# Layer 1's low weight words: sixteen scalings that may run on GpSimd as well as on ScalarE

## The chip, the core and the metric

The kernel runs on one core of a Trainium2 chip. The time is device microseconds of one execution, as the median of several runs. The engines are named as the profile names them: PE is TensorE, PEld its weight loads, DVE is VectorE, ACT is ScalarE, POOL is GpSimd, and SP issues the transfers.

## What is computed

Windowed attention (4 sequences of 576 tokens, 8 heads of 64, window 64) is followed by two layers over all 2304 tokens with a model width of 512 and an inner width of 2048:

```
x = attention(q, k, v)                # 2304 x 512
h = maximum(x @ w1_in, 0); x = (h * h) @ w1_out
h = x @ w2_in; out = (h * cos(h)) @ w2_out
```

The weights reach the device as float64. The matmuls run in a split form: each operand is kept as a high part and a low part in a reduced float32 type, and three products (high·high, high·low, low·high) are added.

## The kernel before

**Weights.** Each layer's weights come in 16 blocks of 128 inner columns. A block is 1 MB of raw float64 in a tile `raw`, 128 partitions by 1024 numbers of two 32-bit words. `convert_w` (line 264) turns it into float32 and splits it. For layer 1 (`dst is None`) these are the steps of a block, all of 128x1024:

- load `raw` (L276, issued on SP);
- `o0`, the high words rescaled on ACT (L287);
- `o1`, the low words scaled by 2^-29 and rounded to integers, in place, on ACT (L245, with integer types in the trace);
- `o2`, the high words shifted left into `cw` on DVE (L299);
- `o4`, the two words added as integers on DVE (L303), which is the float32 weight;
- `hi`, the high part W rounded on ACT (L245, output fp32r);
- `lo`, the low part W by subtraction on DVE (L323).

Layer 2's blocks go through the same steps up to `o4` and are then stored to DRAM as float32 (`dst` is set); they come back later. Below, w0 to w15 are layer 1's raw blocks and W0 to W15 the finished ones.

**Items.** PE's work in layer 1 is a row of items. Item i multiplies one weight block with 256 or 512 tokens into `ph` (L877, 12 matmuls), ACT and DVE form the square `g` as two parts (L597, L601, L605 on ACT, L610 on DVE for the low part), and two items later PE multiplies `g_i` with the block's other half into `accA` (L624, L685). Items 0 to 11 are half units of 256 tokens over blocks 0 to 5, where tokens 0 to 255 start before tokens 256 to 511; from item 12 on, an item is 512 tokens with blocks 6 to 15. The attention of the first two token groups, n = 0 and 1, each in two head groups g, runs ahead of this. `mm` is its row minimum (L481 on DVE), `pb` the exponentials (L487 on ACT, L497 on DVE), T the transposes, O the result, and X the token matrix that `ph` reads.

**Order.** No engine chooses at run time. A planner (`Plan.run`) places every operation on one of the engines its table allows, by estimated costs in us, keys and free buffers, and the program is emitted in that order. `act_us`, `dve_us` and `pool_us` are its costs. Every engine works its instructions off in order. The planner puts an operation that two engines may take where it would be finished first. A different choice for one operation therefore changes the order of many others on all engines.

```
def pool_us(n, two=False):
    return 0.17 + n * (0.0021 if two else 0.00083)
...
        o0 = op({"ACT": act_us(2 * DM)}, key, c0, [o_ld], use=[rb])
        o1 = op({"ACT": act_us(2 * DM)}, key, c1, [o_ld], use=[rb])
```

`copy` (line 243) is the helper that carries out `o1` on whichever engine it is given: an activation on ACT, a `tensor_scalar` with two multiplications on POOL (line 247).

Of the kernel before, what the change touches and what calls it, by code (L numbers as in the profile page):

```python
# [28 lines left out]
def f32(ap):  # L29
    return ap.bitcast(F32)  # L30
# [55 lines left out]
class Plan:  # L86
# [6 lines left out]
    def op(self, engs, key, fn, deps=(), take=(), use=(), lat=None):  # L93
        if lat is None:
            lat = self.PE_LAT if "PE" in engs else self.LAT
        o = Op(engs, key, fn, [d for d in deps if d is not None], list(take), lat)
        o.seq = len(self.ops)
        self.ops.append(o)
        for b in (*take, *use):
            b.users.append(o)  # L100
        return o
# [61 lines left out]
def act_us(n, sbuf=True):  # L163
    return 0.05 + 0.093 * sbuf + n / 1200.0


def dve_us(n, fast=False):
    return 0.065 + n / (1920.0 if fast else 960.0)


def pool_us(n, two=False):
    return 0.17 + n * (0.0021 if two else 0.00083)
# [7 lines left out]
def kernel(  # L180
# [21 lines left out]
    DM = 512  # L202
# [22 lines left out]
    op = plan.op  # L225
# [11 lines left out]
    def dma(key, fn, nbytes, deps=(), take=(), use=(), n=1, order=()):  # L237
        return op({"SP": max(0.6 * n, nbytes / 360e3)}, key, fn, [*deps, *order], take, use, lat=2.2)
# [4 lines left out]
    def copy(e, o, i, scale=1.0):  # L243
        if e == "ACT":
            nc.scalar.activation(o, i, AF.Copy, scale=scale)  # L245
        elif e == "POOL":
            nc.gpsimd.tensor_scalar(o, i, scale, 1.0, ALU.mult, ALU.mult)
        elif scale == 1.0:
            nc.vector.tensor_copy(o, i)
        else:  # L250
            nc.vector.tensor_scalar(o, i, scale, None, ALU.mult)
# [9 lines left out]
    def new_w(wb, nm):  # L261
        wb.tile = wp.tile([P, 2, 2, DM], F32R, tag=f"W{wb.slot}", name=f"W_{nm}")

    def convert_w(src, j, key, after=None, dst=None, early=None):

        nm = f"{src.tensor.name}_{j}"  # L270
        raw, rb = {}, R["W"].buf()
        wb = R["W"].buf() if dst is None else None

        def ld(e):
            raw["t"] = wp.tile([P, 2, DM, 2], I32, tag=f"W{rb.slot}", name=f"raw_{nm}")
            nc.sync.dma_start(  # L276
                raw["t"].rearrange("p a n two -> p (a n two)"), src[j].bitcast(I32))

        o_ld = dma(key - 3 if early is None else early, ld, P * 2 * DM * 8, [after], [rb])

        def words():
            t = raw["t"].rearrange("p a n two -> p (a n) two")
            return t[:, :, 0], t[:, :, 1]

        def c0(e):
            hw = words()[1].bitcast(F32)
            nc.scalar.activation(hw, hw, AF.Prelu, scale=2.0**-112, alpha=-(2.0**32))  # L287

        def c1(e):
            lw = words()[0]  # L290
            copy(e, lw, lw.bitcast(U32), 2.0**-29)

        o0 = op({"ACT": act_us(2 * DM)}, key, c0, [o_ld], use=[rb])
        o1 = op({"ACT": act_us(2 * DM)}, key, c1, [o_ld], use=[rb])
        s, tb = {}, R["w"].buf()

        def c2(e):
            s["w"] = cv.tile([P, 2 * DM], I32, tag="w", name=f"cw_{nm}")
            nc.vector.tensor_scalar(s["w"], words()[1], 3, None, ALU.logical_shift_left)  # L299

        def c4(e):
            w = words()[1] if dst is None else s["w"]
            nc.vector.tensor_tensor(w, s["w"], words()[0], ALU.add)  # L303

        def w32():
            if dst is None:
                return raw["t"].bitcast(F32)[:, :, :, 1]
            return s["w"].bitcast(F32).rearrange("p (a n) -> p a n", a=2)

        o2 = op({"DVE": dve_us(2 * DM, True)}, key, c2, [o0], [tb], use=[rb])  # L310
        o4 = op({"DVE": dve_us(2 * DM)}, key, c4, [o2, o1], use=[rb, tb])
        if dst is None:
            tb = rb
        if dst is not None:
            return [dma(key, lambda e: nc.sync.dma_start(dst[j], w32()), P * 2 * DM * 4, [o4],
                        use=[tb])]

        def c5(e):
            new_w(wb, nm)
            copy(e, wb.tile[:, :, 0], w32())  # L320

        def c6(e):
            nc.vector.tensor_tensor(  # L323
                wb.tile[:, :, 1], w32(), f32(wb.tile[:, :, 0]), ALU.subtract)

        hi = op({"ACT": act_us(2 * DM)}, key, c5, [o4], [wb], [tb])
        lo = op({"DVE": dve_us(2 * DM)}, key, c6, [hi], use=[tb, wb])
        w_hi[j] = [hi, hi]
        w_lo[j] = [lo, lo]
        w_buf[j] = wb  # L330
# [580 lines left out]
    for j in range(NJ):  # L911
        convert_w(w1, j, -6.0 + 2.0 * (j if j < SK else 2 * j - SK), w_lo[j - 4][1] if j >= 4 else None, early=-96.0 + 1.5 * j if j < 2 else None)
# [11 lines left out]
    for i in range(len(items) + LAG + 1):  # L924
# [12 lines left out]
        if i in w2_at:  # L937
            j = w2_at[i]
            w2_done[j] = convert_w(w2, j, pos + 5.0, line[0], w2d)
# [80 lines left out]
```

## Time and profile before

| | |
|---|---|
| median of 3 runs | 886.24 us (886.02 to 887.07) |
| the profiled execution | 886.27 us, span 884.5 us |
| PE busy | 862.2 us, 97% of the span |
| ACT busy | 471.1 us, 53% |
| DVE busy | 509.8 us, 58% |
| POOL busy | 5.0 us, 1%, 25 instructions |

The span is the time from the first to the last instruction on the engines; 1.77 us of the execution lie around it. Busy time of PE counts a matmul from its start to a modelled end, so that a busy PE can still be a slow one; its granted clock stands beside it in some rows, as a share of 2.4 GHz.

### The profile page before, as it was taken

The numbers are of one execution on the slowest core, as the hardware profiler recorded it, in microseconds if no ns is written. First come the engines' busy times: TensorE is split into PE (matmuls) and PEld (weight loads), VectorE is DVE, ScalarE is ACT, GpSimd is POOL, SyncE is SP. The second block draws the span as 40 slices with busy tenths as digits, with TensorE's granted clock in tenths as the row PEclk, the third lists the DMA queues.
The fourth block names the chain that finished last, engine by engine and source line by source line (L and its number), as shares of the span: only waits on it lengthen the run. The fifth ranks groups of instructions, "written<-read, shape, count | busy, mean of one in ns | idle before, by whom it ended". The sixth has DMA issues, their size and how long they took to land.

```text
span 884.5 us, 13320 instructions
## 1 busy us (share of the span) xinstructions
PE 862.2 (97%) x5184; PEld 724.9 (82%) x5184; DVE 509.8 (58%) x1137; ACT 471.1 (53%) x953; POOL 5.0 (1%) x25
## 2 busy tenths in 40 slices
PE   5799999999999999999999999999999999999998
PEld 4698778998788888888888888888888888888897
DVE  4887845424444344434544966676667666766675
ACT  6899966746656655654433533344334333433444
POOL 2000000000000000000000000000000000000000
PEclk8799999999999999999999999999999999999999
DMA  8862236243334343225522200020002000200000
GB/s 329 362 228 96 84 117 223 97 168 137 132 130 161 111 177 128 96 72 160 221 96 95 84 13 1 0 86 11 1 1 95 1 1 1 71 1 1 15 34 25
DMA packets 22655, 85.40 MB, mean 97 GB/s; under 512 B 2368, under 2 KB 3392, under 8 KB 18496
## 3 DMA queue, kind: packets, MB, share of 16 engines
q1 hardware_dynamic: 22592, 84.55, 27.0%
q8 instruction: 41, 0.67, 0.3%
q14 instruction: 22, 0.18, 0.1%
HBM read 66.72 MB, written 17.83 MB: 96 GB/s over the span
## 4 chain that ended last, share of the span: by engine, by line
PE 91%; ACT 6%; DVE 1%; issue 1%; DMA 0%; ACTq 0%
PE ph L877 42%; PE accB L803 22%; PE accA L624 20%; PE S L468 2%; PE O L519 2%; PE T L505 2%; ACT raw_in_w_dram L287 1%; ACT W_in_w_dram L245 1%; ACT raw_in_w_dram L245 1%; ACT g L601 1%; ACT pb L487 1%; ACT r L597 0%; ACT r L605 0%; DMA qk<-in_qk_dram 0%; DVE pb L497 0%
## 5 line engine op out<-in xcount | busy, mean ns | idle before, releaser
L877 PE MATMUL ph<-X,W_in_w_dram 128*128 128x512 f32 (+1 forms) x1032 | 220.6, 360 | 2.5 <-ACT X L554 0.8
L877 PE MATMUL ph<-X,W 128*128 128x512 f32 (+1 forms) x960 | 209.8, 368 | 0.0
L803 PE MATMUL accB<-W,gb 128*128 128x512 f32 x864 | 208.8, 390 | 0.0
L624 PE MATMUL accA<-g,W_in_w_dram 128*128 128x512 f32 (+1 forms) x888 | 200.5, 370 | 0.0
L877 PEld LDWEIGHTS ph<-X,W_in_w_dram 128*128 128x128 f32 x1032 | 172.6, 190 | 32.4 <-issue 1.4
L877 PEld LDWEIGHTS ph<-X,W 128*128 128x128 f32 x960 | 169.3, 188 | 31.2
L803 PEld LDWEIGHTS accB<-W,gb 128*128 128x128 f32 x864 | 161.1, 188 | 32.9 <-ACT gb L780 0.2
L624 PEld LDWEIGHTS accA<-g,W_in_w_dram 128*128 128x128 f32 x888 | 153.2, 189 | 27.3 <-issue 0.9
L753 ACT ACTIVATE u<-ph,quarter 128x512 f32<-128x512 f32 (+1 forms) x80 | 51.7, 646 | 149.0 <-PE ph L877 149.0
L610 DVE TENSOR_TENSOR g<-r,g 128x512 fp32r<-128x512 f32 (+1 forms) x86 | 51.9, 604 | 107.8 <-ACT r L605 107.0
L757 DVE TENSOR_SCALAR u<-u 128x512 f32<-128x512 f32 (+1 forms) x80 | 32.0, 400 | 121.2 <-ACT u L753 121.2
L780 ACT ACTIVATE gb<-rr 128x512 fp32r<-128x512 f32 (+1 forms) x80 | 47.2, 590 | 83.9 <-DVE rr L775 83.9
L601 ACT ACTIVATE g<-r 128x512 fp32r<-128x512 f32 (+1 forms) x86 | 48.3, 561 | 80.3 <-PE accA L624 78.9
L597 ACT ACTIVATE r<-ph 128x512 f32<-128x512 f32 (+1 forms) x86 | 44.9, 522 | 51.6 <-PE ph L877 51.4
L487 ACT ACTIVATE pb<-pb,mm 128x128 f32<-128x128 f32 x144 | 55.9, 390 | 12.7 <-DVE mm L481 12.7
L772 ACT ACTIVATE u<-rr,hpi 128x512 f32<-128x512 f32 (+1 forms) x80 | 53.7, 672 | 0.3 <-DVE rr L768 0.2
L761 DVE SCALAR_TENSOR_TENSOR rr<-u,ph 128x512 f32<-128x512 f32 (+1 forms) x80 | 50.8, 635 | 2.5
L775 DVE TENSOR_TENSOR rr<-ph,u 128x512 f32<-128x512 f32 (+1 forms) x80 | 50.5, 631 | 1.4 <-ACT u L772 1.2
L783 DVE TENSOR_TENSOR gb<-rr,gb 128x512 fp32r<-128x512 f32 (+1 forms) x80 | 50.5, 632 | 1.0 <-ACT gb L780 1.0
L765 DVE SCALAR_TENSOR_TENSOR rr<-u,rr 128x512 f32<-128x512 f32 (+1 forms) x80 | 50.4, 631 | 0.3
L605 ACT ACTIVATE r<-r 128x512 f32<-128x512 f32 (+1 forms) x84 | 47.1, 561 | 2.7
L287 ACT ACTIVATE raw_in_w_dram<-raw_in_w_dram 128x1024 f32<-128x1024 f32 x32 | 36.7, 1147 | 1.7 <-DMA raw_in_w_dram<-in_w_dram 1.7
(63 smaller groups left out, 575.7 us busy)
## 6 DMA issues: line engine op xcount, KB each, us to landing
raw_in_w_dram<-in_w_dram SPq DMA_DIRECT2D x32, 1024.0 KB, 6.7
qk<-in_qk_dram SPq DMA_DIRECT2D x18, 576.0 KB, 4.1
v<-in_v_dram SPq DMA_DIRECT2D x18, 512.0 KB, 3.6
w_dram<-cw_in_w_dram SPq DMA_DIRECT2D x16, 512.0 KB, 3.8
w<-w_dram SPq DMA_DIRECT2D x8, 1024.0 KB, 5.0
x_dram<-x SPq DMA_DIRECT2D x18, 256.0 KB, 2.2
out_dram<-o SPq DMA_DIRECT2D x18, 256.0 KB, 2.0
xr<-x_dram SPq DMA_DIRECT2D x16, 256.0 KB, 2.7
```

The costliest lines, as they stand in the source:

```text
L487: nc.scalar.activation(t["pb"][:, e, r, i], t["pb"][:, e, r, i], AF.Exp, bias=t["mm"][:, e, r, i:i + 1], scale=-1.0, accum_out=t["sm"][:, ...
L601: nc.scalar.activation(t["g"][:, 0], t["r"], AF.Square)
L610: nc.vector.tensor_tensor(t["g"][:, 1], t["r"], f32(t["g"][:, 0]), ALU.subtract)
L624: nc.tensor.matmul(self.acc[i][:, k, :], w[:, 1, wl, m * P:m * P + P], t["g"][:, gl, :], start=(j == 0 and p == 0 and k == 0 and self.n > ...
L753: nc.scalar.activation(t["u"], ph()[:, 0:w], AF.Identity, bias=quarter, scale=INV_2PI)
L761: nc.vector.scalar_tensor_tensor(t["r"], t["u"], -C1, ph()[:, 0:w], ALU.mult, ALU.add)
L765: nc.vector.scalar_tensor_tensor(t["r"], t["u"], -C2, t["r"], ALU.mult, ALU.add)
L772: nc.scalar.activation(t["u"], t["r"], AF.Sin, bias=hpi)
L775: nc.vector.tensor_tensor(t["r"], ph()[:, 0:w], t["u"], ALU.mult)
L783: nc.vector.tensor_tensor(t["g"][:, 1], t["r"], f32(t["g"][:, 0]), ALU.subtract)
L803: nc.tensor.matmul(self.acc[m], t["g"][:, gl, m * P:m * P + P], w[:, 1, wl], start=(j == 0 and k == 0), stop=(j == NJ - 1 and k == 2))
L877: nc.tensor.matmul(t["ph"][:, 0:u.w], wb.tile[:, 0, wl, c * P:c * P + P], u.x(xl, c), start=(c == 0 and k == 0), stop=(c == NCC - 1 and k ...
```

## The change

Operation `o1` of layer 1's blocks may now run on POOL too, at a planner's cost of 0.17 + 1024 x 0.00083 + 0.15 = 1.17 us. Layer 2's blocks keep ACT alone.

```diff
-        o1 = op({"ACT": act_us(2 * DM)}, key, c1, [o_ld], use=[rb])
+        low = {"ACT": act_us(2 * DM)}
+        if dst is None:
+            low["POOL"] = pool_us(2 * DM) + 0.15
+        o1 = op(low, key, c1, [o_ld], use=[rb])
```

In the order that results, all sixteen of these operations stand on POOL and none on ACT, and lines behind the change move down by 3 (L299 becomes L302, and so on). SP issues the load of w5 one place earlier, ahead of an attention load. PE's order is the same up to the first `ph` and close to it for the items after. Three places follow.

DVE, from the sum of w2 to that of w3, while the attention of n = 1, g = 1 begins. Before (the rows left out are the other seven row minima of the same kind):

```order
L303 ISA raw_in_w1_dram_2_255<-raw_in_w1_dram_2_255,cw_in_w1_dram_2_415 128x1024x2
L323 TENSOR_TENSOR W_in_w1_dram_1_420<-raw_in_w1_dram_1_209,W_in_w1_dram_1_420 128x2x512
L481 ISA pb_1_1_424,mm_1_1_454<-S_1_1_0_425,row_mask_n_106 128x128
...
L323 TENSOR_TENSOR W_in_w1_dram_2_452<-raw_in_w1_dram_2_255,W_in_w1_dram_2_452 128x2x512
L493 TENSOR_SCALAR sm_1_1_455<-sm_1_1_455 128x4
```

With the change:

```order
L306 ISA raw_in_w1_dram_2_257<-raw_in_w1_dram_2_257,cw_in_w1_dram_2_406 128x1024x2
L613 TENSOR_TENSOR g_0_452<-r_0_431,g_0_452 128x256
L302 TENSOR_SCALAR cw_in_w1_dram_3_463<-raw_in_w1_dram_3_347 128x1024
L484 ISA pb_1_1_433,mm_1_1_471<-S_1_1_0_434,row_mask_n_106 128x128
...
L326 TENSOR_TENSOR W_in_w1_dram_2_458<-raw_in_w1_dram_2_257,W_in_w1_dram_2_458 128x2x512
L496 TENSOR_SCALAR sm_1_1_472<-sm_1_1_472 128x4
L497 RECIPROCAL sm_1_1_472<-sm_1_1_472 128x4
L500 TENSOR_TENSOR pb_1_1_433<-pb_1_1_433,sm_1_1_472 128x512
L306 ISA raw_in_w1_dram_3_347<-raw_in_w1_dram_3_347,cw_in_w1_dram_3_463 128x1024x2
```

The low part of g_0 and the shift of w3 now stand ahead of the eight row minima, and the low part of W1 has moved ahead of the sum of w2.

ACT, from the square of item 2 on, up to X for the second half's last head group. Before:

```order
L245 ACTIVATE raw_in_w1_dram_3_344<-raw_in_w1_dram_3_344 128x1024
L601 ACTIVATE g_2_556<-r_2_535 128x256
L605 ACTIVATE r_2_535<-r_2_535 128x256
L287 ACTIVATE raw_in_w1_dram_4_401<-raw_in_w1_dram_4_401 128x1024
L554 ACTIVATE X_83<-O_1_1_559 128x2x256
```

With the change:

```order
L604 ACTIVATE g_2_551<-r_2_545 128x256
L608 ACTIVATE r_2_545<-r_2_545 128x256
L287 ACTIVATE raw_in_w1_dram_4_408<-raw_in_w1_dram_4_408 128x1024
L287 ACTIVATE raw_in_w1_dram_5_455<-raw_in_w1_dram_5_455 128x1024
L287 ACTIVATE raw_in_w1_dram_6_499<-raw_in_w1_dram_6_499 128x1024
L557 ACTIVATE X_83<-O_1_1_571 128x2x256
```

Three rescalings of high words stand in a row before X, where one stood before.

DVE, behind X of the second half, up to g_6. With the change:

```order
L560 TENSOR_TENSOR X_83<-O_1_1_571,X_83 128x2x256
L302 TENSOR_SCALAR cw_in_w1_dram_5_596<-raw_in_w1_dram_5_455 128x1024
L326 TENSOR_TENSOR W_in_w1_dram_4_594<-raw_in_w1_dram_4_408,W_in_w1_dram_4_594 128x2x512
L306 ISA raw_in_w1_dram_5_455<-raw_in_w1_dram_5_455,cw_in_w1_dram_5_596 128x1024x2
L302 TENSOR_SCALAR cw_in_w1_dram_6_633<-raw_in_w1_dram_6_499 128x1024
L306 ISA raw_in_w1_dram_6_499<-raw_in_w1_dram_6_499,cw_in_w1_dram_6_633 128x1024x2
L613 TENSOR_TENSOR g_3_631<-r_3_608,g_3_631 128x256
L326 TENSOR_TENSOR W_in_w1_dram_5_642<-raw_in_w1_dram_5_455,W_in_w1_dram_5_642 128x2x512
L326 TENSOR_TENSOR W_in_w1_dram_6_660<-raw_in_w1_dram_6_499,W_in_w1_dram_6_660 128x2x512
L613 TENSOR_TENSOR g_4_670<-r_4_654,g_4_670 128x256
```

Before, the same stretch held less weight work between two items:

```order
L610 TENSOR_TENSOR g_3_615<-r_3_596,g_3_615 128x256
L323 TENSOR_TENSOR W_in_w1_dram_4_626<-raw_in_w1_dram_4_401,W_in_w1_dram_4_626 128x2x512
L303 ISA raw_in_w1_dram_5_461<-raw_in_w1_dram_5_461,cw_in_w1_dram_5_620 128x1024x2
L610 TENSOR_TENSOR g_4_652<-r_4_635,g_4_652 128x256
L299 TENSOR_SCALAR cw_in_w1_dram_6_677<-raw_in_w1_dram_6_492 128x1024
L323 TENSOR_TENSOR W_in_w1_dram_5_679<-raw_in_w1_dram_5_461,W_in_w1_dram_5_679 128x2x512
L610 TENSOR_TENSOR g_5_691<-r_5_675,g_5_691 128x256
```

Weight work has moved forward on DVE: between g_3 and g_12 it now holds nine low parts (L323), eight shifts (L299) and eight sums (L303).

## Rows read from the trace of the kernel before

**Rows 1.** Busy time per stretch: start:end, length, engines, PEclk, DMA share, GB/s.

```profile
30.00:40.00 10.00, 8.33 (x84) 7.11 (x81) 9.32 (x28) 8.66 (x25) 0.00 (x0) 0.84 0.80 320
...
50.00:60.00 10.00, 10.00 (x85) 10.00 (x84) 8.00 (x10) 9.87 (x18) 0.00 (x0) 1.00 0.46 164
...
150.00:884.50 734.50, 730.62 (x4025) 611.88 (x4017) 405.45 (x870) 347.01 (x678) 0.00 (x0) 1.00 0.22 75
```

**Rows 2.** PE in order of time: start, us, engine, line, [idle before <-releaser].

```profile
36.74 0.50 PE L877 MATMUL ph<-X,W_in_w_dram 128*128 128x256 f32 x2 [0.41 <-ACT W_in_w_dram L245]
38.00 1.10 PE L877 MATMUL ph<-X,W_in_w_dram 128*128 128x256 f32 x7 [0.76 <-DVE W_in_w_dram L323]
39.52 1.09 PE L505 MATMUL T<-ident,pb 128*128 128x128 f32 x4 [0.42 <-ACT pb L487]
...
46.47 0.38 PE L877 MATMUL ph<-X,W_in_w_dram 128*128 128x256 f32 x1 [0.79 <-ACT X L554]
47.32 0.86 PE L877 MATMUL ph<-X,W_in_w_dram 128*128 128x256 f32 x5 [0.46 <-DVE X L557]
...
53.77 1.60 PE L685 MATMUL accA<-g,W_in_w_dram 128*128 128x256 f32 x12
55.20 1.60 PE L877 MATMUL ph<-X,W_in_w_dram 128*128 128x256 f32 x12
...
83.59 2.88 PE L624 MATMUL accA<-g,W_in_w_dram 128*128 128x512 f32 x12
```

**Rows 3.** The same view, at 151 us, behind layer 1's last weight block.

```profile
151.49 1.60 PE L877 MATMUL ph<-X,W_in_w_dram 128*128 128x256 f32 x12
152.93 1.60 PE L624 MATMUL accA<-g,W_in_w_dram 128*128 128x256 f32 x12
```

**Rows 4.** PE alone per microsecond: start:end, length, busy (instructions), granted clock, DMA.

```profile
41.00:42.00 1.00, 1.00 (x7) 0.50 0.99 418
...
49.00:50.00 1.00, 1.00 (x11) 1.00 0.89 344
```

**Rows 5.** ACT in order of time: r_0's last step, one o1, then w4's rescaling and X.

```profile
34.23 0.42 ACT L605 ACTIVATE r<-r 128x256 f32<-128x256 f32 x1
...
42.16 1.14 ACT L245 ACTIVATE raw_in_w_dram<-raw_in_w_dram 128x1024 int32<-128x1024 uint32 x1
...
43.99 0.42 ACT L601 ACTIVATE g<-r 128x256 fp32r<-128x256 f32 x1 [0.69 <-PE accA L685]
...
44.76 1.18 ACT L287 ACTIVATE raw_in_w_dram<-raw_in_w_dram 128x1024 f32<-128x1024 f32 x1
45.83 0.59 ACT L554 ACTIVATE X<-O 128x512 fp32r<-128x512 f32 x1
```

**Rows 6.** DVE in order of time: first row minimum, W2's low part, X, then one block's steps.

```profile
34.74 0.28 DVE L481 CUSTOM_DVE_ANT_0 pb<-S,row_mask_n 128x128 f32<-128x128 f32 x1
...
36.72 1.23 DVE L323 TENSOR_TENSOR W_in_w_dram<-raw_in_w_dram,W_in_w_dram 128x1024 fp32r<-128x1024 f32 x1 [0.21 <-ACT W_in_w_dram L245]
...
46.58 0.68 DVE L557 TENSOR_TENSOR X<-O,X 128x512 fp32r<-128x512 f32 x1
...
59.26 0.69 DVE L299 TENSOR_SCALAR cw_in_w_dram<-raw_in_w_dram 128x1024 int32<-128x1024 int32 x1
60.01 0.43 DVE L610 TENSOR_TENSOR g<-r,g 128x256 fp32r<-128x256 f32 x1
61.05 1.23 DVE L323 TENSOR_TENSOR W_in_w_dram<-raw_in_w_dram,W_in_w_dram 128x1024 fp32r<-128x1024 f32 x1 [0.62 <-ACT W_in_w_dram L245]
62.39 1.23 DVE L303 CUSTOM_DVE_ANT_0 raw_in_w_dram<-raw_in_w_dram,cw_in_w_dram 128x2048 uint16<-128x2048 uint16 x1
```

**Rows 7.** POOL in order of time: three of its 25 instructions, all before 6.6 us.

```profile
4.17 0.20 POOL masks.py:197 MEMSET ident<- 128x128 f32 x1
4.44 0.29 POOL masks.py:199 TENSOR_SCALAR_AFFINE_SELECT ident<-ident 128x128 f32<-128x128 f32 x1
4.68 0.10 POOL L391 MEMSET hpi<- 128x1 f32 x1
```

## The prediction

> **What bounds the kernel now.** I read the busy time per stretch first, then PE in order of time. From 150 us on PE idles 3.9 us in 734.5, all of it behind the last matmul; between 50 and 60 us it does not idle [rows 1]. Up to the first `ph` the attention of the first tokens and its loads set the pace; PE's order there is unchanged, and the change takes nothing from that chain. So nearly all of PE's idle time that a weight conversion could cause lies between the first `ph` and 48 us: waits of 0.41, 0.76, 0.42, 0.79 and 0.46 us, together 2.84 us [rows 2]. In part of that stretch PE is also slow: at a granted clock of 0.50 it does 7 matmuls in a microsecond, at 1.00 it does 11 [rows 4].
>
> ACT is the engine that looks full: 9.87 us of 10 from 50 to 60 us [rows 1]. But it does not hold PE there. Twelve matmuls of 256 columns take 1.43 us in that stretch (53.77 to 55.20) [rows 2], and 1.44 us at 151 us, where layer 1's weight work is long over [rows 3]. PE runs at its own pace in both places. From 48 us on the kernel's end is therefore the moment at which the second half's `ph` gets its X (47.32 us [rows 2]) plus a sum of matmuls that the change leaves alone, unless something new makes PE wait.
>
> **What the change removes.** Sixteen instructions of about 1.14 us on ACT [rows 5], some 18 us of its time. Behind 48 us this is worth nothing by itself, because PE is the bound there. Ahead of 48 us three or four of them stand among the work that PE waits for, so I replayed the new order with the old durations. Consecutive DVE instructions overlap a little: eight row minima of 0.28 us took 36.72 - 0.21 - 34.74 = 1.77 us, so I take 0.07 off each duration as its step [rows 6].
>
> - Low part of W2. In the new order g_0's low part and the shift of w3 come ahead of the eight row minima. g_0 needs r_0, done at 34.23 + 0.42 = 34.65 us [rows 5]; with 0.36 and 0.62 us behind it, the minima begin at about 35.6 instead of 34.74 us, and W2's low part at 35.6 + 1.8 = 37.4 instead of 36.72 us [rows 6]. `ph` of item 2, which resumed at 38.00 us, resumes at about 38.6. The transpose behind it started at 39.52 us, late because of exponentials on ACT [rows 2]; now it starts at about 39.7, behind the matmuls. The wait for W2's high part (0.41 us) goes, and this one takes its place.
> - X of the second half. Its O is needed first, and the T and O before it are on PE as late as before. On ACT, w4's, w5's and w6's rescaling now come in a row ahead of it. w4's began at 44.76 us; without the 1.07 us step of `o1` that stood ahead of it and without the 0.69 us wait behind that, it begins at 43.0, and three steps of about 1.03 us end at 46.1 us; X then ends at 46.8 instead of 45.83 + 0.59 = 46.42 us [rows 5]. DVE has w4's sum before X's low part, which ends at about 47.7 us instead of 46.58 + 0.68 = 47.26 [rows 6]. What was saved on ACT is spent by work drawn forward.
>
> Term one: PE's uninterrupted run begins about 0.4 us later.
>
> **What it adds.** Sixteen POOL instructions of 128x1024, two words apart, from unsigned to signed integers. The trace has no such row. From below: a MEMSET grows from 0.10 us for 1 column to 0.20 for 128, which gives 0.91 us for 1024 columns by a straight line. From above: AFFINE_SELECT, which reads and writes, takes 0.29 us for 128 columns; with the same 0.10 us of start this gives 1.63 us for 1024 [rows 7]. The new operation reads and writes like the second but tests no pattern per element; I take 1.2 us. The GPSIMD Engine Reference of the Trainium skill, section 7, states about 1.9 cycles an element for reads of at most 8 bytes a step, at 1.2 GHz; the estimate from that page is 1.6 us, and with it the sum below would be 894.7 us. No run here shows it yet.
>
> As a producer POOL hides at any of these prices: it has nothing else to do and starts when a load has landed, where `o1` stood in line on ACT. What is open is whether it holds DVE up. In every stretch of [rows 1] POOL has no instruction, so no row shows the two at work on SBUF together. Bounds: such a pair costs DVE nothing, or the whole POOL instruction, 1.2 us. It costs nothing if the two have separate ways to SBUF. One row speaks for a shared one: DVE's shift passes 1024 words in 0.69 us, its subtraction 1024 in 1.23 [rows 6], so what DVE gets out of SBUF depends on the form of the instruction, and it sometimes takes more than one way. I take the upper bound for instructions that stand among DVE's weight steps, and keep zero as the rival.
>
> The page "SBUF — State Buffer" of the Trainium skill, section "SBUF: two separate sides", says that the two engines share a pair of ports as an exclusive lock, held for a whole instruction, against DVE instructions in a two-port mode or with two SBUF inputs. By that rule the upper bound holds, and L299, L303, L323 and L610 all come under it; without it the sum would end at term one, 886.7 us. Before this change the trace neither agrees nor disagrees.
>
> Term two, 29 to 48 us. Six loads land here, so about six POOL instructions run (w4 to w9). DVE is busy 9.32 us of 10 from 30 to 40 [rows 1], but in the replay it also has waits that swallow some: w2's sum ends near 33.4 us, and g_0 cannot start before 34.65 [rows 5]. I choose to count one of the six as late on the path, on W2's low part or the normalisation behind it: 1.2 us.
>
> Term three, behind 48 us. DVE now has its weight work packed. From X's low part (47.7) five steps come before g_3: 0.62 + 1.16 + 1.16 + 0.62 + 1.16 = 4.7 us, so g_3's low part ends at 52.8. PE wants it 6.45 us after X, as before (53.77 - 47.32 [rows 2]), at 54.15: slack 1.35 us. From g_3 to g_12 DVE has nine L323 of 1.16, eight L299 of 0.62, eight L303 of 1.16 and nine L610 of 0.36: 10.4 + 5.0 + 9.3 + 3.2 = 27.9 us, while PE takes 83.59 - 53.77 = 29.8 us [rows 2]. Spare: 1.9 us. The six POOL instructions that are left (w10 to w15) run in this stretch, as buffers come free. If each takes its 1.2 us out of DVE, 7.2 us stand against 1.35 + 1.9 = 3.25, and g's low parts reach PE 3.95 us late. PE does not make this up. Without turn-taking, term three is zero: the cover is that spare.
>
> **Sum.** 0.4 + 1.2 + 3.95 = 5.5 us on the profiled execution's 886.27 us (0.03 above the median of the runs): **891.8 us**. At the upper bound of 1.63 us a POOL instruction, with two on the early path: 0.4 + 3.3 + 6.5 = 10.2, 896.5 us. At no cost at all: 886.7 us.
>
> **Rivals.** About 0.2%, 1.8 us, is what a measurement of this kernel tells from no change.
>
> - *The cover holds* (0.30). POOL and DVE do not disturb each other, or only at L299, with the subtractions and sums free: eight shifts between g_3 and g_12 lose half a microsecond each at most, 4 us against a spare of 3.25. Time 886.7 us, from 885.5 to 888. For it: POOL has 99% of the span free, DVE has slack. Against: DVE is packed, so even small losses add up.
> - *Faster* (0.13). ACT relieved lets the conversions arrive early enough that PE's waits of 2.84 us between 36 and 48 us go, and PE, without these gaps, does not fall to clock 0.50 [rows 4]. This would be worth up to 2.84 us and, for that slow microsecond and its neighbours, an estimated 1.6 more: 881.9 us, or 883.4 with the waits alone. For it: ACT is named in two of the five waits. Against: the replay, where other work moves into each gap. It decides if the minima on DVE do not wait for g_0.
> - *Worse* (0.07). The POOL instruction costs 2.3 us (AFFINE_SELECT's 0.29 times eight) and DVE takes turns with it: term three is 6 x 2.3 - 3.25 = 10.6, with 0.4 and two of 2.3, about 15.6: 901.9 us.
> - That the scheduler leaves them on ACT is ruled out by the order.
>
> **How the numbers follow.** The forecast, turn-taking at 0.9 to 1.63 us, has a chance of 0.50: it spans about 888.5 to 896.5 us. Slower is that and the worst case, 0.57; within 0.2% is the cover, 0.30; faster is 0.13. The range runs from 884.6 to 897.0 us: it takes in the cover case with an error of the replay of 2 us, and leaves out the worst case and nearly all of the faster one, 0.19.
>
> **What would show it.** Right: POOL rows of about 1.2 us or longer beside DVE rows; L299, L303 or L323 longer than 0.69 and 1.23 us, or DVE idle before L303 for POOL; PE waits for DVE's g (L613) between 55 and 85 us; DVE close to 10 of 10 there. X's low part near 47.7 us or later. Wrong: DVE's durations as before under POOL's rows, PE without a wait behind 48 us (then 886.7), or PE's waits between 36 and 48 us gone (then less). A clock that falls at another place than around 41 us would move the start by up to 1.6 us either way.

## The result: 894.27 us, 0.9% slower, and the profile after

The changed kernel takes 894.27 us (median of 4 runs, 893.88 to 894.59) against 886.13 us for the kernel before on the same chip (4 runs): a ratio of 1.0092, 95% interval 1.0077 to 1.0106. It is 8.1 us slower where 5.5 us were forecast; 894.27 lies inside the range. Line numbers of the changed kernel are 3 higher behind the diff (L299 is L302, L303 is L306, L323 is L326, L610 is L613).

What answers to [rows 1], busy time per stretch of the changed kernel (start:end, length, PE, PEld, DVE, ACT, POOL, PEclk, DMA share, GB/s):

```profile
30.00:40.00 10.00, 7.71 (x90) 6.69 (x89) 10.00 (x25) 6.99 (x20) 3.30 (x2) 0.80 0.86 308
...
50.00:60.00 10.00, 8.45 (x59) 8.30 (x59) 9.83 (x10) 6.92 (x12) 3.15 (x3) 0.83 0.62 212
...
150.00:892.40 742.40, 738.54 (x4113) 618.59 (x4111) 410.15 (x878) 354.71 (x693) 0.00 (x0) 1.00 0.22 76
```

ACT is relieved, as the change meant: 6.99 instead of 8.66 us in the stretch from 30 to 40. DVE, which got no work, goes from 9.32 to 10.00 of 10 there and from 8.00 to 9.83 between 50 and 60. PE's idle time behind 150 us is what it was, 3.9 us. The loss lies ahead of that, and PE in order of time shows where (compare [rows 2]):

```profile
28.74 1.09 PE L508 MATMUL T<-ident,pb 128*128 128x128 f32 x4 [3.55 <-DVE pb L500]
...
32.41 2.79 PE L880 MATMUL ph<-X,W_in_w_dram 128*128 128x256 f32 x15
...
40.25 1.34 PE L880 MATMUL ph<-X,W_in_w_dram 128*128 128x256 f32 x7 [2.06 <-DVE W_in_w_dram L326]
...
49.76 0.39 PE L880 MATMUL ph<-X,W_in_w_dram 128*128 128x256 f32 x1 [0.80 <-ACT X L557]
51.70 1.43 PE L880 MATMUL ph<-X,W_in_w_dram 128*128 128x256 f32 x5 [1.55 <-DVE X L560]
52.93 2.32 PE L688 MATMUL accA<-g,W_in_w_dram 128*128 128x256 f32 x12
55.09 1.60 PE L880 MATMUL ph<-X,W_in_w_dram 128*128 128x256 f32 x12
...
73.81 1.98 PE L688 MATMUL accA<-g,W_in_w_dram 128*128 128x256 f32 x12
...
77.65 1.57 PE L688 MATMUL accA<-g,W_in_w_dram 128*128 128x256 f32 x11 [0.30 <-DVE g L613]
...
91.40 2.83 PE L627 MATMUL accA<-g,W_in_w_dram 128*128 128x512 f32 x11 [0.85 <-DVE g L613]
```

X's low part lets PE go on at 51.70 instead of 47.32 us: 4.4 us late. The next twelve `accA` matmuls pass in 2.16 us (52.93 to 55.09; the granted clock is 0.50 between 52 and 54 us), where at clock 1.00 they need 1.44, and the five `ph` ahead of them in 1.23 instead of 0.69: 1.3 us more, so 5.6 us are lost by 55. Three `accA` groups then start before DVE's low part of g is ready: the one at 73.81 takes until 75.63, 1.82 us instead of 1.44, the one at 77.07 takes 1.99 instead of 1.44, the one at 90.16 takes 4.01 instead of 2.82 (83.59 to 86.41 before). That is 2.1 us, of which 1.15 show as waits for g. By 94 us 7.8 us are lost, nearly the whole of it. Apart from the 0.80 us for X's high part on ACT, the waits shown here name DVE.

DVE's longer rows lie beside POOL's. POOL, then DVE, of the changed kernel in order of time:

```profile
26.94 1.10 POOL L247 TENSOR_SCALAR raw_in_w_dram<-raw_in_w_dram 128x1024 int32<-128x1024 uint32 x1 [6.79 <-DMA raw_in_w_dram<-in_w_dram]
...
48.55 1.43 POOL L247 TENSOR_SCALAR raw_in_w_dram<-raw_in_w_dram 128x1024 int32<-128x1024 uint32 x1 [0.40 <-issue]
```

```profile
27.09 0.18 DVE L497 RECIPROCAL sm<-sm 128x4 f32<-128x4 f32 x1
27.30 1.29 DVE L500 TENSOR_TENSOR pb<-pb,sm 128x512 f32<-128x512 f32 x1
...
49.15 1.89 DVE L306 CUSTOM_DVE_ANT_0 raw_in_w_dram<-raw_in_w_dram,cw_in_w_dram 128x2048 uint16<-128x2048 uint16 x1
50.97 0.68 DVE L560 TENSOR_TENSOR X<-O,X 128x512 fp32r<-128x512 f32 x1
```

Alone, a POOL instruction takes 1.10 us. The normalisation (L500, 0.69 us undisturbed) that starts at 27.30 ends at 28.59; POOL's instruction ends at 28.04, and 0.55 us later DVE's is done. The sum at 49.15 (1.22 us undisturbed) ends at 51.04, 1.06 us behind POOL's end at 49.98. Both look as if DVE's instruction had done most of its work only after POOL's was over. X's low part stands behind that sum, and PE behind X.

### The profile page after: what moved, and what is told of

It reads as the page before. It is cut to its first block, busy times and chain, and to the rows that moved or that the text cites. A ratio compares the mean times of both kernels' runs of the same rounds, so it can differ in the third digit from the quotient of the medians.

```text
span 892.4 us, 13342 instructions
## 1 busy us (share of the span) xinstructions
PE 865.2 (97%) x5184; PEld 726.9 (81%) x5184; DVE 518.2 (58%) x1138; ACT 457.1 (51%) x936; POOL 27.5 (3%) x41
## 4 chain that ended last, share of the span: by engine, by line
PE 88%; DVE 3%; issue 1%; ACT 1%; DVEq 0%; ACTq 0%
PE ph L880 42%; PE accB L806 22%; PE accA L627 20%; PE O L522 2%; PE S L471 2%; PE T L508 1%; DVE W_in_w_dram L326 1%; DVE raw_in_w_dram L306 1%; DVE cw_in_w_dram L302 1%; DVE g L613 0%; ACT pb L490 0%; ACT r L600 0%; ACT g L604 0%; ACT r L608 0%; ACT o L827 0%
## 5 line engine op out<-in xcount | busy, mean ns | idle before, releaser
L613 DVE TENSOR_TENSOR g<-r,g 128x512 fp32r<-128x512 f32 (+1 forms) x86 | 54.0, 628 | 111.7 <-ACT r L608 111.5
L778 DVE TENSOR_TENSOR rr<-ph,u 128x512 f32<-128x512 f32 (+1 forms) x80 | 50.5, 631 | 1.4 <-ACT u L775 1.3
L786 DVE TENSOR_TENSOR gb<-rr,gb 128x512 fp32r<-128x512 f32 (+1 forms) x80 | 50.5, 631 | 1.1 <-ACT gb L783 1.0
```

The lines of the kernel that those rows point to most:

```text
L613: nc.vector.tensor_tensor(t["g"][:, 1], t["r"], f32(t["g"][:, 0]), ALU.subtract)
L778: nc.vector.tensor_tensor(t["r"], ph()[:, 0:w], t["u"], ALU.mult)
L786: nc.vector.tensor_tensor(t["g"][:, 1], t["r"], f32(t["g"][:, 0]), ALU.subtract)
```

## The experiments

The theory after the result: POOL and DVE take turns at SBUF, a whole instruction at a time (theory 1). The rival: the new order costs the time, because it draws weight work forward past what PE wants next (theory 2). A third possibility, that DVE waits for what POOL produces, falls with the trace of the changed kernel: none of DVE's waits between 7 and 100 us is for POOL. The first four runs separate order and occupancy; the next four look for the place of each; the last two try to get the loss back. Each has five rounds. The kernel before, on the same chips, took 886.31, 886.38 and 886.55 us in the three groups.

**new_order_small**: the order of the change, and hardly any work on POOL. The sum on DVE reads zeros, so that it doesn't depend on POOL either.

```diff
+            if e == "POOL":
+                lw = lw[:, 0:16]
...
-            nc.vector.tensor_tensor(w, s["w"], words()[0], ALU.add)
+            nc.vector.tensor_tensor(
+                four(w), four(s["w"]), zero.unsqueeze(1).to_broadcast([P, 4, DM // 2]), ALU.add)
```

> The changed kernel's order on every engine, with the sixteen POOL instructions cut from 1024 columns to 16 and the integer sum on DVE reading a row of zeros in place of the scaled low words (so the weights lack their low words). Theory 1, turn-taking: POOL keeps DVE out of SBUF for as long as its instruction lasts. With 16 columns nearly nothing is left of that: no DVE row of L302, L306, L326 above 0.7, 1.25 and 1.25 us, and the time falls back to 886.7 us (885.5 to 888). Theory 2, the order: weight work drawn forward on DVE and ACT delays g and X by itself. Then it stays near 894 us (above 891).

Measured: 889.41 us, ratio 1.0032 (1.0020 to 1.0045), 3.1 us over the kernel before. DVE's sums and differences are back at 1.23 us and PE waits for nothing between 54 and 100 us. So part of the loss is order alone, and far more than the 0.4 us of term one. ACT, then PE, of this run:

```profile
43.84 0.42 ACT L613 ACTIVATE g<-r 128x256 fp32r<-128x256 f32 x1 [1.48 <-PE accA L697]
...
44.61 3.21 ACT L288 ACTIVATE raw_in_w_dram<-raw_in_w_dram 128x1024 f32<-128x1024 f32 x3
47.72 0.58 ACT L566 ACTIVATE X<-O 128x512 fp32r<-128x512 f32 x1
```

```profile
48.35 0.38 PE L889 MATMUL ph<-X,W_in_w_dram 128*128 128x256 f32 x1 [1.89 <-ACT X L566]
49.08 0.86 PE L889 MATMUL ph<-X,W_in_w_dram 128*128 128x256 f32 x5 [0.34 <-DVE X L569]
49.77 2.66 PE L697 MATMUL accA<-g,W_in_w_dram 128*128 128x256 f32 x12
52.23 2.07 PE L889 MATMUL ph<-X,W_in_w_dram 128*128 128x256 f32 x12
```

The rescalings begin at 44.61, not at the forecast 43.0, and hardly earlier than before (44.76 [rows 5]). `o1` is gone from ACT, but the wait for `accA` that followed it grew from 0.69 to 1.48 us: g_2 needs a buffer that PE gives back at its own time, and `o1` had only filled that wait. Three rescalings then take until 47.7 where one took until 45.8. X is 1.9 us late on ACT, and PE resumes at 49.08 instead of 47.32, 1.8 us late. Behind that longer wait the granted clock falls to 0.50 between 50 and 53 us; `accA` and `ph` pass in 4.36 us (49.77 to 54.13) instead of 2.87 (48.01 to 50.88 before), another 1.5. 1.8 + 1.5 = 3.3 us.

POOL's rows of this run show the turn-taking from the other side, with an instruction of 16 columns:

```profile
9.54 0.21 POOL L248 TENSOR_SCALAR raw_in_w_dram<-raw_in_w_dram 128x16 int32<-128x16 uint32 x1 [2.73 <-DMA raw_in_w_dram<-in_w_dram]
...
43.00 1.27 POOL L248 TENSOR_SCALAR raw_in_w_dram<-raw_in_w_dram 128x16 int32<-128x16 uint32 x1 [2.04 <-issue]
```

The same instruction takes 0.21 us alone and 1.27 us when it comes 0.01 us behind the start of a DVE difference of 1.21 us (42.99): it waits for the whole of it.

**old_order_pool**: PE, DVE and SP in the order of before, word for word; the low words scaled by POOL.

```diff
-            copy(e, lw, lw.bitcast(U32), 2.0**-29)
+            copy("POOL" if dst is None else e, lw, lw.bitcast(U32), 2.0**-29)
```

> The order of the kernel before on PE, DVE and SP, word for word; only the sixteen scalings are issued on POOL, and ACT simply lacks them. Theory 1, turn-taking: DVE's rows stretch as in the changed kernel (up to about 2.2 us), the attention and the first items are late by some 4 us, and DVE, less packed behind 48 us, adds under 2: 890 to 892 us. Theory 2, the order: nothing is drawn forward, POOL is harmless and ACT is relieved: 886 us or less.

Measured: 890.23 us, ratio 1.0036 (1.0022 to 1.0050), 3.9 us over, without any change of order. PE of this run:

```profile
29.11 1.09 PE L505 MATMUL T<-ident,pb 128*128 128x128 f32 x4 [3.52 <-DVE pb L497]
...
32.88 2.63 PE L877 MATMUL ph<-X,W_in_w_dram 128*128 128x256 f32 x12
...
50.87 0.87 PE L877 MATMUL ph<-X,W_in_w_dram 128*128 128x256 f32 x5 [1.35 <-DVE X L557]
51.58 2.35 PE L685 MATMUL accA<-g,W_in_w_dram 128*128 128x256 f32 x12
...
55.94 1.60 PE L685 MATMUL accA<-g,W_in_w_dram 128*128 128x256 f32 x12
```

All of it is lost ahead of 56 us. The last T ahead of `ph` waits 3.52 us instead of 2.85 for its normalisation, PE waits 1.35 instead of 0.46 for X's low part, and it resumes at 50.87, 3.6 us late. Behind that wait the granted clock falls here too (0.50 between 53 and 55 us): the twelve `accA` and the twelve `ph` pass in 4.36 us (51.58 to 55.94) instead of 2.87, another 1.5. Between 54 and 100 us PE has no wait. What turn-taking costs thus contains a slow stretch, which no run separates from it.

**old_order_small**: the old order with the 16 columns and the zeros.

```diff
+            if dst is not None:
+                nc.vector.tensor_tensor(w, s["w"], words()[0], ALU.add)
+                return
...
+            if dst is None:
+                e, lw = "POOL", lw[:, 0:16]
```

> As the run above, with 16 columns on POOL and zeros for the low words: ACT relieved, nothing on POOL that could hold DVE up, and the old order. Both theories: this is what the change could have brought at most in this order. My replay says the waits of 0.41 and 0.79 us for ACT shrink and others stay: 885 to 886.2 us. The rival of the prediction that ACT is what holds PE between 36 and 48 us: 882 to 884 us.

Measured: 886.04 us, ratio 0.9993 (0.9984 to 1.0002). Here ACT does sixteen instructions less, nothing else is disturbed, and the time is that of before. The kernel does not feel ACT's 18 us.

The four corners, in us:

| | 16 columns on POOL | full size on POOL |
|---|---|---|
| order of before | 886.0 | 890.2 |
| order of the change | 889.4 | 894.3 |

Order costs 3.4 to 4.0, occupancy 4.2 to 4.9, and together they make 8.2 (8.1 in the pair of the result). Each of the two single changes has a slow stretch of 1.5 us behind X in its trace, and the changed kernel has one of 1.3. So these sums are not prices of waiting alone, and that they nearly add up doesn't show the two to be independent.

**new_order_twice**: the changed kernel, and every POOL instruction followed by a second one of the same size (times 1).

```diff
+            if e == "POOL":
+                copy(e, lw, lw)
```

> The changed kernel with each POOL scaling followed by a second POOL pass over the same words (times 1). Theory 1, turn-taking: sixteen more POOL instructions of 1.1 us, with DVE busy 9.6 to 10 of 10 from 30 to 90 us: 8 to 16 us more than the changed kernel, 902 to 910 us. Theory 2, the order: POOL has room, so 894 to 895 us.

Measured: 907.19 us, ratio 1.0236 (1.0222 to 1.0250), 12.9 us over the changed kernel: sixteen instructions more, 0.8 us each by division. This is not waiting alone: from 30 to 60 us the mean granted clock is 0.50 to 0.67 here, against 0.80 to 0.83 in the changed kernel. That DVE is what PE waits for is shown by PE's waits up to 110 us (us in total, times, longest; the first of them is 5.6 us in 4 waits in the kernel before):

```profile
PE T L510 <- DVE pb L502: 13.3, 6, 3.7
...
PE accA L629 <- DVE g L615: 2.5, 1, 2.5
```

**old_pool_w0_3, old_pool_w4_9, old_pool_w10_15**: the order of before, and only these blocks' low words on POOL.

```diff
-            copy(e, lw, lw.bitcast(U32), 2.0**-29)
+            copy("POOL" if dst is None and j < 4 else e, lw, lw.bitcast(U32), 2.0**-29)
```

> Order of the kernel before; the low words of blocks 0 to 3 alone go to POOL at full size, the other twelve stay on ACT. Theory A, the early instructions hold DVE's normalisations, sums and differences up, on which the first ph hangs: the first ph starts 1.6 to 2.0 us later than 30.86 us and the loss is carried to the end, 887.6 to 888.6 us. Theory B, as the prediction had it (the chain of the first tokens loses nothing): 885.9 to 886.6 us.

Measured: 888.91 us, ratio 1.0031 (1.0019 to 1.0043). Four instructions beside the attention of the first tokens cost 2.5 us. POOL and DVE of this run, where the last normalisation ahead of the first `ph` is made:

```profile
27.19 1.38 POOL L247 TENSOR_SCALAR raw_in_w_dram<-raw_in_w_dram 128x1024 int32<-128x1024 uint32 x1 [7.09 <-DMA raw_in_w_dram<-in_w_dram]
```

```profile
27.53 1.07 DVE L493 TENSOR_SCALAR sm<-sm 128x4 f32<-128x4 f32 x1
```

An instruction of 4 columns, 0.17 us elsewhere, takes 1.07 and ends 0.03 us behind POOL's. The first `ph` starts at 33.45 us, 2.6 late. In the rows, two holds of this instruction make 1.4 of it (0.63 us at 9.15, and the one shown); the other 1.2 pass around a stretch at clock 0.50 that lasts from 12 to 22 us, where before it ended at 19. Whether POOL lengthened that stretch is not shown: in the changed kernel, with the same four instructions, the clock stays at 1.00 from 8 to 27 us.

> Order of the kernel before; blocks 4 to 9 alone on POOL at full size. Theory A, each place where DVE is held ahead of X's low part counts by itself: first ph unchanged at 30.9 us, X's low part and with it PE's last wait 1.2 to 2.0 us later than 47.32 us, 887.4 to 888.6 us. Theory B, the waits of DVE between its steps in this stretch swallow the holds as long as the start is not late: 885.9 to 886.8 us.

Measured: 889.32 us, ratio 1.0029 (1.0020 to 1.0039); nine runs from 886.87 to 889.86. Six instructions between 30 and 50 us cost some 2.6 us by the ratio, a little above theory A's range. The profiled execution took 887.65, well under the median, so its rows show places and not the size of the loss. DVE, then PE:

```profile
37.97 2.04 DVE L323 TENSOR_TENSOR W_in_w_dram<-raw_in_w_dram,W_in_w_dram 128x1024 fp32r<-128x1024 f32 x1
```

```profile
40.06 1.16 PE L877 MATMUL ph<-X,W_in_w_dram 128*128 128x256 f32 x7 [1.73 <-DVE W_in_w_dram L323]
```

PE's wait for W2's low part is 1.73 us where it was 0.76 [rows 2]. Together the two parts make 5 us where all sixteen made 3.9 (old_order_pool): they don't add in full. Why was not tried.

> Order of the kernel before; blocks 10 to 15 alone on POOL at full size. Theory A, DVE's spare behind 50 us covers six held instructions: PE without a wait behind 48 us, 885.6 to 886.8 us, although L299, L303 and L323 rows up to 2.2 us show. Theory B, as term three of the prediction had it, the holds exceed the spare and g's low parts come late: PE waits for g between 55 and 90 us, 888 to 890 us.

Measured: 886.54 us, ratio 0.9999 (0.9990 to 1.0008): no loss, although DVE is held as before. POOL, DVE and PE of this run:

```profile
51.98 2.10 POOL L247 TENSOR_SCALAR raw_in_w_dram<-raw_in_w_dram 128x1024 int32<-128x1024 uint32 x1 [45.44 <-DMA raw_in_w_dram<-in_w_dram]
```

```profile
53.18 1.98 DVE L303 CUSTOM_DVE_ANT_0 raw_in_w_dram<-raw_in_w_dram,cw_in_w_dram 128x2048 uint16<-128x2048 uint16 x1
```

```profile
18.82 1.97 PE L519 MATMUL O<-PT,v 128*64 128x64 f32 x32
...
31.86 2.93 PE L877 MATMUL ph<-X,W_in_w_dram 128*128 128x256 f32 x12
...
47.49 0.86 PE L877 MATMUL ph<-X,W_in_w_dram 128*128 128x256 f32 x5 [0.47 <-DVE X L557]
```

A caution comes with it. The first `ph` starts 1.0 us later than before although POOL does nothing here between 6.6 and 51.98 us. The trace of before has this O row as follows:

```profile
18.58 1.32 PE L519 MATMUL O<-PT,v 128*64 128x64 f32 x32
```

The same 32 matmuls take 0.65 us longer, at a granted clock of 0.50 in that stretch. By 47.49 us the delay is gone but for 0.17 us, because the clock stays at 1.00 from 36 us on, where before it falls to 0.50 around 41 [rows 4]. In a single trace, a shift of up to 1 us at the first `ph` need not be the change's; for sizes the medians of five rounds are used.

**new_order_x_first**: new_order_small with one swap on ACT, X ahead of the third rescaling (w6's). `late` is set on that rescaling, `mark` on X.

```diff
+        early = [x for x in order if getattr(x[1], "late", False)]
+        for x in early:
+            order.remove(x)
+            k = next(i for i, y in enumerate(order) if getattr(y[1], "mark", False))
+            order.insert(k + 1, x)
```

> Order of the changed kernel with the small POOL instruction and the zeros, as in new_order_small (889.4 us), and one swap on ACT: X of the second half comes ahead of the third of the three rescalings that stood in a row in front of it. Theory A, the order's cost sits in those rescalings, which begin late because of the wait for accA, and in the low clock behind PE's wait for X: X starts about 1.1 us earlier (46.6 instead of 47.72 us), PE's wait of 1.89 us for it shrinks to about 0.8, and the time is 886.8 to 888.4 us, the lower end if the slow microseconds behind the wait go too. Theory B, the cost sits earlier, in the wait of 2.32 us for W2's low part, and the rescalings only fill time that is lost anyway: 889.0 to 889.8 us.

Measured: 888.00 us, ratio 1.0018 (1.0009 to 1.0027), 1.4 us less than without the swap (its slowest execution, 888.57, lies below the fastest without, 888.84). ACT, then PE:

```profile
46.40 0.59 ACT L572 ACTIVATE X<-O 128x512 fp32r<-128x512 f32 x1
```

```profile
47.04 0.38 PE L896 MATMUL ph<-X,W_in_w_dram 128*128 128x256 f32 x1 [0.87 <-ACT X L572]
48.12 0.86 PE L896 MATMUL ph<-X,W_in_w_dram 128*128 128x256 f32 x5 [0.69 <-DVE X L575]
48.81 2.16 PE L704 MATMUL accA<-g,W_in_w_dram 128*128 128x256 f32 x12
```

X starts 1.3 us earlier and PE resumes 1.0 us earlier, as theory A had it. The clock still falls behind it (0.50 between 50 and 52 us), and the rest of the order's cost stays: 1.6 us.

**after_x_first**: the same swap in the changed kernel, POOL at full size.

> The changed kernel with one swap on ACT: X of the second half ahead of the third rescaling that stood in front of it; POOL at full size. Theory A, the order's cost and the turn-taking add up: the swap is worth here what it was with the small POOL instruction (1.4 us), 892.3 to 893.3 us against 894.3. Theory B, with POOL at full size DVE's holds (X's low part, W2's low part) come last before PE resumes and the swap on ACT is hidden: 893.8 to 894.6 us.

Measured: 894.73 us, ratio 1.0093 (1.0079 to 1.0107), as without the swap. Here the rescalings are not what X waits for: with one of them moved behind it, ACT sits idle 1.16 us until PE delivers O, and X starts at 49.06 instead of 49.14. PE's second wait, 1.67 us for DVE's low part of X, ends last. ACT, then PE:

```profile
49.06 0.60 ACT L563 ACTIVATE X<-O 128x512 fp32r<-128x512 f32 x1 [1.16 <-PE O L528]
```

```profile
51.76 0.86 PE L887 MATMUL ph<-X,W_in_w_dram 128*128 128x256 f32 x5 [1.67 <-DVE X L566]
```

In front of that low part stands the sum of w4, which lasts 1.90 instead of 1.22 us beside POOL. POOL holds up both kinds, but where the old order had w4's shift (0.70 us) directly ahead of the instruction that PE wants, the new order has w4's sum. So at full size the order's cost does not lie in the rescalings, as it did in new_order_small.

**low_on_dve**: ACT relieved without POOL. The planner may give the low words to DVE, and gives it ten of the sixteen.

```diff
-            low["POOL"] = pool_us(2 * DM) + 0.15
+            low["DVE"] = dve_us(2 * DM, True)
```

> ACT is relieved without POOL: the low words may go to DVE (its 2x form, about 0.69 us as L299) or ACT, as the scheduler finds; ten of sixteen go to DVE, so the order is a new one. Theory A, ACT's relief is worth nothing wherever the work goes, and a new order costs what it puts ahead of PE's next input: no gain, 886 to 890 us. Theory B, a relieved ACT without turn-taking does let PE's waits between 36 and 48 us go: 883 to 885.3 us, which would beat both kernels.

Measured: 888.90 us, ratio 1.0025 (1.0016 to 1.0034). There is no turn-taking, but this order too has rescalings in front of X. ACT of this run:

```profile
45.63 2.26 ACT L287 ACTIVATE raw_in_w_dram<-raw_in_w_dram 128x1024 f32<-128x1024 f32 x2
47.77 0.58 ACT L557 ACTIVATE X<-O 128x512 fp32r<-128x512 f32 x1
```

X starts at 47.77, as late as in new_order_small, and the granted clock falls behind it here too (0.50 between 51 and 53 us). PE also waits 2.57 us for W2's low part. Which of the two counts was not tried. No version here beats the kernel before: the two that cost nothing, old_order_small and old_pool_w10_15, gain nothing either.

## Why the prediction was right or wrong

**Right: the sign, and the mechanism of term two and term three.** PE at its own pace behind 48 us where nothing holds it, ACT's relief worth nothing (old_order_small), and turn-taking as the price (old_order_pool, new_order_twice) all held. The faster rival falls with old_order_small. "The cover holds" is true for blocks 10 to 15 in the old order (old_pool_w10_15) and false for the changed kernel.

The rule of the Trainium skill that the prediction weighed ("SBUF — State Buffer", section "SBUF: two separate sides": an exclusive lock for whole instructions, against DVE instructions in a two-port mode or with two SBUF inputs) agrees with the trace. L302, L306, L326, L500 and L613 are all held, by up to 1.0 us. Instructions that read PSUM are not: row minima beside POOL's instruction of 19.02 to 20.15 us keep their length, as this row of the changed kernel shows.

```profile
19.44 0.29 DVE L484 CUSTOM_DVE_ANT_0 pb<-S,row_mask_n 128x128 f32<-128x128 f32 x1
```

The reciprocal of 128x4 isn't held either, though it works from SBUF to SBUF: at 27.09 it takes its usual 0.18 us inside POOL's instruction of 26.94 to 28.04.

**Right: the price.** 1.2 us were taken for a POOL instruction, between 0.91 and 1.63; it is 1.10 us where nothing disturbs it. The estimate of 1.6 us from section 7 of the Trainium skill's GPSIMD Engine Reference does not fit; the measurement decides.

**Wrong: term one, 0.4 us; new_order_small measured 3.1.** The step that failed is "without the 1.07 us step of `o1` that stood ahead of it and without the 0.69 us wait behind that, it begins at 43.0". `o1` and the wait do not both go. The end of the wait is a moment on PE (the `accA` matmuls that free g's buffer), so taking `o1` away only lengthened the wait, 0.69 to 1.48. ACT then had three rescalings ahead of X, with no time saved to pay for them. The replay of W2's low part in the same term was right: `ph` of item 2 was to resume at about 38.6, and did at 38.78 in new_order_small. The low clock behind the longer wait, about 1.5 us, was named at the end of the prediction ("would move the start by up to 1.6 us") but stood in no term.

**Wrong: "the change takes nothing from that chain", the attention ahead of the first `ph`.** The order there is unchanged, but the first four POOL instructions lie beside its normalisations, sums and differences. Alone they cost 2.5 us (old_pool_w0_3), of which the rows show 1.4 as holds. The prediction applied turn-taking "for instructions that stand among DVE's weight steps" and left L496 and L500, which read SBUF too, out of it.

**Too small: term two, 1.2 us for blocks 4 to 9.** old_pool_w4_9 measured 2.6. The prediction counted one of the six as late on the path. In old_pool_w4_9's trace more than one lies on DVE's work there: W2's low part takes 2.04 us, a normalisation (L497) 1.36 instead of 0.69 and the sum ahead of X 1.56 instead of 1.22. How much of each reached PE is shown only for the first.

**Too large: term three, 3.95 us; about 2.1 us in the changed kernel.** The form was right: six POOL instructions against a spare of 3.25 us. DVE's groups between 50.5 and 94 us, with their mean ns:

```profile
L306 DVE CUSTOM_DVE_ANT_0 raw_in_w_dram<-raw_in_w_dram,cw_in_w_dram 128x2048 uint16<-128x2048 uint16 x12 | 16.1, 1340 | 1.5
L326 DVE TENSOR_TENSOR W_in_w_dram<-raw_in_w_dram,W_in_w_dram 128x1024 fp32r<-128x1024 f32 x11 | 15.1, 1384 | 0.0
L302 DVE TENSOR_SCALAR cw_in_w_dram<-raw_in_w_dram 128x1024 int32<-128x1024 int32 x11 | 8.0, 729 | 0.1
L613 DVE TENSOR_TENSOR g<-r,g 128x256 fp32r<-128x256 f32 x9 | 5.6, 626 | 0.0
```

Against 1.224, 1.224, 0.692 and 0.421 us before these are 1.4 + 1.8 + 0.4 + 1.8 = 5.4 us more. Without the sum at 49.15, which began ahead of this stretch (0.7 us), 4.7 us are left for six instructions: 0.8 us each, not 1.2. Less the spare of 3.25, that is 1.45 us, where the three `accA` groups lost 2.1; the spare was replayed and not measured, so the rest stays open. That the sum of the prediction came near, 5.5 against 8.1, was luck: term three was 1.9 us too large, while the early part, 1.6 us forecast and 5.6 lost, was 4 too small, and 1.3 of those 5.6 are the low clock behind X, for which the sum had no term.

## What to carry to other kernels

An engine that looks idle is not free if it reads the same memory as the one beside it: count each of its instructions as a possible hold on every neighbour whose operands lie in SBUF, small ones included (here only the reciprocals went free), from the first instruction on and not only where the change rewrites the order. When you replay an order by hand, find out for each wait what ends it: an instruction that stood inside a wait gives nothing back when it goes. And when a freed engine draws later work forward, look for what that work now stands in front of.

## What the runs showed of the hardware that was not expected

- The wait goes both ways and is visible as length: POOL's 16-column instruction takes 0.21 us alone and up to 1.28 us beside DVE (new_order_small); the full one 1.10 alone and up to 2.22 (old_order_pool). A POOL row's length is not its work.
- A DVE instruction of 128x4, 0.17 us long, was held for 1.07 us (old_pool_w0_3).
- The granted clock's low stretches fall at other places from one execution to the next and can move the first `ph` by 1 us without moving the end (old_pool_w10_15). The low stretch behind X came in the runs in which PE had waited longer for X: 1.89 + 0.34 us in new_order_small, 0.69 + 1.35 in old_order_pool, 0.80 + 1.55 in the changed kernel; not after 0.92 + 0.47 in old_pool_w10_15. No run was made to test a cause.
